# A spectral network's convolutions in quarter tiles of TensorE, with the complex products summed there or from turned matrices

## The chip, the core and the metric

One core of a Trainium2 chip. The metric is the device time of one execution in microseconds. The engines are TensorE (PE, with its weight loads PEld), VectorE (DVE), ScalarE (ACT), GpSimd (POOL) and SyncE (SP), whose queue issues most of the DMAs. "Partition" is the row of on-chip memory (SBUF, and PSUM for TensorE's results, in banks of 128 partitions by 512 float32).

## What is computed

```python
x = A_x                                    # 1 x 2048 x 512, float32
x = x + A(layernorm(x), w_r, w_i)          # A: irfft2(rfft2(x) * (w_r + i w_i))
x = x + B(layernorm(x), ...)               # B: along the 2048 rows, channel by channel:
x = x + A(layernorm(x), w_r, w_i)          #   y = irfft(rfft(u, 4096) * rfft(K, 4096))[:2048] + u * D_skip
x = x + B(layernorm(x), ...)               #   K = 2 Re sum_n C[d, n] exp(dt A[d, n])^position
```

The B layer is a long convolution. Its kernel K (512 channels, 2048 positions, 128 terms each) depends on the parameters alone and is the same in both B layers.

## The kernel before

**The stages**, by the times of the profiled execution: to 76 us the input is normalized and K's parameters are made; to 250 the first A layer runs beside the first half of K; to 456 the second half of K runs beside blocks 0 and 1 of the first B layer; to 546 the rest of that layer; to 663 the second A layer; to 785 the second B layer.

**K in time** (`kernel_time`) goes by 64 half-units in eight groups. `grow` makes powers (`mag`), `bend` multiplies phases on TensorE and rounds them on VectorE (L840, into `kw`), `sine` and `cosine` are ScalarE's (L805), `terms` multiplies on VectorE (L859, L861, into `qp`), `total` sums on TensorE (L872, into `pv`). ScalarE copies the sums to `stage` (L879), and after the last half of a group four DMAs write `stage` to `kt` in DRAM (L883, 128 KB each, SP's queue).

**A convolution** (`forward_b`, `layer_b`) goes by four blocks of 128 channels. Steps of a block:
- `rows`, four times: the first stage of the Fourier transform, small matmuls of 64 x 64 tiles (in the trace `p<-t,w` and `p<-t,x`), copied by ScalarE to `z` (L651).
- `turn`, eight times: VectorE transposes `z` in 32 x 32 pieces (L657).
- `pair` and `weigh`, four times: for each of two planes (real and imaginary part) two or three matmuls of 64 columns with a constant matrix from `mb` (`p<-z,mb`, one PSUM bank a plane) give 16 frequencies of a channel on each half of the partitions; VectorE multiplies each plane by both planes of the kernel's spectrum `kk` (L963, four products into `wb`), and two sums of 64 partitions each make the complex product in `u` (L975, on GpSimd or VectorE as the tables YB and YC say: "v" is VectorE). Frequency 0 and the one at half the rate, both real, are packed in one element that is multiplied apart (L965, with `kf0`).
- `units`, eight times: 16 matmuls (`p<-mb,u`, 64 columns, 64 elements moved) go back through the inner stage; ScalarE copies to the second `u` (L984 to L988). A small one (L983, matrix MIX) sets right the packed element.
- `rows` back, four times: eight matmuls (`p<-u,t`, 64 columns, 128 elements moved) and VectorE's sum with the residual (L1002, into `za` or `xw`); in the first B layer it also takes the statistics of the next layer norm (L1007).

`kernel_freq` (F) takes K through the same forward steps, block by block. ScalarE copies its planes to `kk` (L926), VectorE sets the packed element apart (L934 to L936), and `kk` goes to DRAM as `kf` (L938, SP's queue). In the first B layer the product reads the tiles `kk` where F left them; in the second they are loaded from `kf`, two DMAs of 256 KB a step.

**What sets the order.** `interleave` merges lists of steps by their place in each list; `layer_b` writes the order of a block's steps out by hand, with K's steps between them (`fill`). A scheduler then sets each engine's order of instructions from the program order and its own estimates. Tiles rotate through pools (`w`, `wb`, `kk`, `u`, `qp`, PSUM's `p1`, `p2`, `p3`): a tile's next use waits until the last reader of the earlier one is done. `p2`, which holds the pair's results, has three banks in most of the first B layer and in the second.

Of the kernel before, what the change touches and what calls it, by code (L numbers as in the profile page):

```python
# [12 lines left out]
ALU = mybir.AluOpType  # L13
# [8 lines left out]
WW = 8  # L22
DQ = ''
# [5 lines left out]
LAGV = 4  # L29
# [21 lines left out]
MAG = 4  # L51
TH = 2
QP = 5
KF = 1
PM = '2,3,0'
WB = 7
YB = 'vgggvggg'
YC = 'vgggvgggvgvgvgvv'
# [27 lines left out]
def constants():  # L86
# [18 lines left out]
    out["tbt"] = (T * (2 / 4096)).transpose(4, 3, 0, 2, 1).reshape(128, 32 * 64)  # L105
# [71 lines left out]
    MB = np.zeros((2, 2, 32, 2, 2, 2, 32))  # L177
    MBT = np.zeros((2, 2, 32, 2, 2, 32))
    MIX = np.zeros((2, 2, 32, 2, 2, 32))
    for dq in range(2):  # L180
        for sp, m in enumerate((M0, M)):
            MB[:, dq, :, sp, :, dq, :] = m.reshape(2, 32, 2, 8, 2, 2).transpose(4, 2, 3, 5, 0, 1).reshape(2, 32, 2, 32)
        MBT[:, dq, :, :, dq, :] = M.transpose(0, 1, 3, 2)
        MIX[:, dq, :, :, dq, :] = mix.transpose(2, 3, 0, 1)
    out["mb"] = np.concatenate([MB.reshape(128, 256), MBT.reshape(128, 128), MIX.reshape(128, 128)], 1)

    k0 = (np.arange(128) % 32 == 0).astype(float)[:, None]
    out["kc"] = np.concatenate([k0, 1 - k0], 1)
# [61 lines left out]
class Net:  # L250
# [22 lines left out]
    @contextmanager  # L273
    def phase(self, name, space=bass.MemoryType.SB, side="left", **tags):

        with self.tc.tile_pool(name=name, bufs=1, space=space, side=side, reuse_waits="tile") as pool:
            for tag, v in tags.items():
                self.tags[tag] = self.tags[v] if isinstance(v, str) else (pool, tag, *v)
            yield
        for tag in tags:  # L280
            del self.tags[tag]

# [103 lines left out]
    def layer_a(self, w, x=None, src=None, dst=None):  # L386
# [76 lines left out]
        def spread_four(n0):  # L463
# [5 lines left out]
            g = [self.even[:, i, n0:n0 + 4] for i in range(2)]  # L469
# [13 lines left out]
            for i in range(4):  # L483
                t = self.sb("kk", [128])
# [143 lines left out]
    def forward_b(self, src, T, tag="z", extra=None):  # L628
# [5 lines left out]
        def rows(n0):  # L634


            if n0 == 0:
# [3 lines left out]
            products = [(ps[b][64 * c:64 * c + 64, :, j, m], xs[2 * m + c][64 * b:64 * b + 64, 64 * j:64 * j + 64],  # L641
                         T[64 * b:64 * b + 64, n0 + 2 * m + c].rearrange("p (u r) -> p u r", r=2))
                        for m in range(2) for j in range(2) for c in range(2) for b in range(2)]
            if extra and n0 == 0:
                e = extra()
                for j in (1, 0):
                    products.insert(4 * j + 1, (ps[0][0:64, :, j, 0], e[:, 64 * j:64 * j + 64], products[0][2], True))
# [11 lines left out]

        MB = split(self.small[:, 0:256], "slm", [2, 2, 64])  # L660

        def pair(i, use):
            last = None
            for pl in range(2):
                p = self.ps("p2", [512])
                products = []
                for h in (1, 0):
                    o = p[64 * h:64 * h + 64].rearrange("p (u d) -> p u d", d=32)
                    u = 32 * (i % 2) + 16 * h
                    c = 1 if u == 0 else 0  # L670
                    z = tiles["zt"][:, :, i // 2]
                    products += [(o[:, 0], MB[:, 0, pl], z[:, 0])] * c + [(o[:, c:], MB[:, 1, pl], z[:, u + c:u + 16])]
# [227 lines left out]
    def kernel_freq(self, blk, kt, d_skip, kf, kept, T):  # L900

        nc = self.nc
        m0, m1 = self.kc[0:64, 0:1], self.kc[0:64, 1:2]
# [16 lines left out]
        rows, turns, pairs = self.forward_b(src, T, extra=skip)  # L920

        def keep(i):
            k = kept[blk, i] = [self.sb("kk", [512]) for pl in range(2)]

            def use(pl, p):
# [302 lines left out]
```

## Time and profile before

| | |
|---|---|
| median of the runs | 787.68 us (786.29 to 788.17) |
| the profiled execution | 786.58 us, of which its span 784.8 |
| mean granted TensorE clock | 0.899 |
| largest busy times | PE 612.4, DVE 646.6, ACT 420.4, POOL 415.4 us |
| DMA | 80.26 MB, mean 102 GB/s |

A profile's times are in microseconds from the start of the span, a single instruction's in ns. Its rows name line, engine, operation, output and inputs, and the shapes as partitions x elements. A granted clock of 0.9 means that the throttle let TensorE run at 0.9 of its full rate. Float32 matmuls leave two records each in the trace; 128*64 in front of a shape is the tile of TensorE (rows * columns).

### The profile page before, as it was taken

To read this page: it belongs to the slowest core of one execution; us is meant where nothing else is said; L and a number is where in the kernel's file an instruction comes from. 1 tells how busy PE (TensorE), PEld (TensorE's weight loads), DVE (VectorE), ACT (ScalarE), POOL (GpSimd) and SP (SyncE) were. 2 spreads that over 40 slices of the span, in tenths; PEclk is the share of its full clock that TensorE was granted. 3 is DMA by queue.
4 is the path that set the end of the run, shared out by engine and by line. 5 is a ranking of instruction groups with operands and counts; after the bars stand their busy time and mean duration, and the time that the engine had idled before them with its cause. 6 is when DMAs were issued, how large, how long until landed. Compare 5 with 4: busy or idle time off the path is not lost. (4 is left out here: it accounts for less than half of the span.)

```text
span 784.8 us, 20886 instructions
## 1 busy us (share of the span) xinstructions
PE 612.4 (78%) x8208; PEld 417.6 (53%) x8208; DVE 646.6 (82%) x1301; ACT 420.4 (54%) x919; POOL 415.4 (53%) x596
## 2 busy tenths in 40 slices
PE   3337788698758687897867977865899897889986
PEld 2336566464424342654343645644877664466666
DVE  7999749889997769968996977878587598789993
ACT  3434788755556676787477833323766335243322
POOL 3675886766625226732675166281055473375850
PEclk9656999998975999899989999997999898799998
DMA  8300651343547232452326359422122004134403
GB/s 320 117 0 1 147 124 49 102 101 129 125 161 148 72 105 49 129 139 79 43 67 146 113 120 252 133 82 81 54 82 83 28 14 147 56 91 128 145 24 105
DMA packets 144257, 80.26 MB, mean 102 GB/s; under 512 B 78656, under 2 KB 123840, under 8 KB 143264
## 3 DMA queue, kind: packets, MB, share of 16 engines
q1 hardware_dynamic: 143904, 78.51, 36.0%
q8 instruction: 65, 1.06, 0.5%
q0 software_dynamic: 256, 0.43, 0.3%
q14 instruction: 32, 0.26, 0.1%
HBM read 54.30 MB, written 25.03 MB: 101 GB/s over the span
## 5 line engine op out<-in xcount | busy, mean ns | idle before, releaser
L975 POOL TENSOR_TENSOR u<-wb,wb 64x512 f32<-64x512 f32 x90 | 137.0, 1523 | 81.2 <-DVE wb L963 74.5
L319 PE MATMUL p<-z,mb 128*64 128x512 f32 (+1 forms) x480 | 104.0, 543 | 13.2 <-DVE wb L963 5.8
L651 ACT COPY z<-p 128x512 f32<-128x512 f32 x96 | 51.5, 595 | 70.5 <-PE p L319 47.0
L861 DVE TENSOR_TENSOR qp<-qp,mag 128x1024 f32<-128x1024 f32 x64 | 83.3, 1305 | 1.2
L963 DVE TENSOR_TENSOR wb<-p,kk 128x512 f32<-128x512 f32 x128 | 80.6, 674 | 4.0 <-PE p L319 4.0
L859 DVE SCALAR_TENSOR_TENSOR qp<-qp,mag 128x256 f32<-128x256 f32 x128 | 63.6, 512 | 18.7 <-ACT qp L805 18.4
L319 PEld LDWEIGHTS p<-mb,u 128*64 128x64 f32 x2048 | 67.6, 146 | 17.9 <-issue 9.6
L319 PE MATMUL p<-mb,u 128*64 128x64 f32 x2048 | 69.9, 231 | 8.6 <-DVE u L975 4.2
L657 DVE STREAM_TRANSPOSE z<-z 128x512 f32<-128x512 f32 x96 | 58.5, 673 | 21.1 <-ACT z L651 21.1
L1087 POOL TENSOR_SCALAR w<-w,norms 128x128 f32<-128x128 f32 x64 | 37.8, 604 | 62.7 <-DMA w<-h 59.7
L530 DVE TENSOR_TENSOR w<-wt,p 128x514 f32<-128x514 f32 x64 | 42.5, 687 | 32.4 <-PE p L319 24.2
L535 POOL TENSOR_TENSOR w<-w,w 64x257 f32<-64x257 f32 x48 | 40.0, 834 | 53.7 <-DVE w L530 45.8
L872 PEld LDWEIGHTS pv<-qp 128*32 128x32 f32 x2048 | 38.0, 120 | 53.8 <-issue 20.2
L805 ACT ACTIVATE kf<-pk 128x512 f32<-128x512 f32 x64 | 38.8, 606 | 48.7 <-PE pk L841 48.4
L459 PE MATMUL p<-w,w 128*128 128x128 f32 x128 | 32.1, 429 | 40.6 <-DVE w L452 30.9
L319 PEld LDWEIGHTS p<-z,mb 128*64 128x64 f32 x480 | 34.4, 142 | 50.5 <-issue 30.9
L319 PE MATMUL p<-t,w 64*64 64x128 f32 x1024 | 48.1, 309 | 16.7 <-DMA w<-kt 8.1
L872 PE MATMUL pv<-qp 128*32 128x64 f32 x2048 | 51.6, 240 | 8.2 <-DVE qp L861 5.3
L988 ACT COPY u<-p 128x512 f32<-128x512 f32 x64 | 37.4, 589 | 38.1 <-PE p L319 38.1
L840 DVE TENSOR_SCALAR kw<-pk 128x512 bf16<-128x512 f32 x64 | 43.0, 679 | 13.3 <-PE pk L839 13.3
L319 PEld LDWEIGHTS p<-t,w 64*64 64x64 f32 x1024 | 36.8, 152 | 29.0 <-DMA w<-kt 10.7
L459 PEld LDWEIGHTS p<-w,w 128*128 128x128 f32 x128 | 27.8, 318 | 44.6 <-issue 24.7
(198 smaller groups left out, 1498.1 us busy)
## 6 DMA issues: line engine op xcount, KB each, us to landing
wt<-in_w SPq DMA_DIRECT2D x32, 257.0 KB
kf<-kk SPq DMA_DIRECT2D x32, 256.0 KB
kk<-kf SPq DMA_DIRECT2D x32, 256.0 KB
u<-in_x SPq DMA_DIRECT2D x16, 256.0 KB
hr<-in_x SPq DMA_DIRECT2D x16, 256.0 KB
kt<-stage SPq DMA_DIRECT2D x32, 128.0 KB
h<-hr SPq DMA_DIRECT2D x16, 256.0 KB
w<-kt SPq DMA_DIRECT2D x32, 128.0 KB
```

The costliest lines, as they stand in the source:

```text
L319: last = self.nc.tensor.matmul(out, weights, data, start=not more, stop=True, skip_group_check=True).ins
L459: nc.tensor.matmul(p[:, b], xf[:, b], t, start=True, stop=True)
L530: nc.vector.tensor_mul(m[pl], W, px[:, None, :].to_broadcast([128, 2, 257]))
L535: e[0].tensor_sub(Y[0:64, v], m[0][hs, 0], m[1][hs, 1])
L651: nc.scalar.copy(tiles["z"][:, :, :, b, m:m + 2].rearrange("p u j m r -> p (u j) (m r)"), ps[b].rearrange("p u j m r -> p (u j) (m r)"))
L657: nc.vector.transpose(tiles["zt"][:, u:u + 8].rearrange("p u j d -> p (u j d)"), tiles["z"][:, u:u + 8].rearrange("p u j b m r -> p (u j b ...
L840: nc.vector.tensor_scalar(whole, p, MAGIC, -MAGIC, op0=ALU.add, op1=ALU.add)
L859: nc.vector.scalar_tensor_tensor(QP[:, c, 0], QP[:, c, 1, :, ::-1], -1.0 if c else 1.0, m[:, 0], op0=ALU.mult, op1=ALU.mult)
L861: nc.vector.tensor_mul(t, t, mag[:, None, 1:3, 256 * j:256 * j + 256].to_broadcast([128, 2, 2, 256]))
L872: nc.tensor.matmul(p[32 * t:32 * t + 32, g], QP[:, c, 2, d], QP[:, c, 0:2, d], start=c == 0, stop=c == 1, tile_position=(0, 32 * t), skip_ ...
L963: nc.vector.tensor_mul(split(m[c, pl], "du", [32, 16]), by_channel(p), split(k[c], "du", [32, 16]))
L975: self.added = e[0].tensor_sub(y[0:64], v[0, 0], v[1, 1]), e[1].tensor_add(y[64:128], v[0, 1], v[1, 0])
```

## The change

**Layout.** The planes now alternate by row: the real and the imaginary part of a frequency lie on neighbouring partitions, so that one tile of 128 partitions holds two channel halves (`q`) or row halves (`j`) of both planes. Every matmul of a convolution works in a quarter of TensorE, 64 x 64 (the forward rows in 64 x 32), and a step writes two PSUM banks where it wrote one.

**The complex product.** In the first B layer (`ADD` False) each result of a pair is multiplied by two versions of the spectrum, real parts in both rows of a couple and imaginary parts in both, straight into two tiles `M[0]` and `M[1]`, and the sum is left to TensorE: `units` accumulates two matmuls, with the matrices `MT[0]` and `MT[1]`. In the second (`ADD` True) a second set of matmuls with turned matrices (`TWI`, i times the first) is multiplied by the imaginary parts, and GpSimd adds the two products, 128 partitions at once. `kk` is loaded from `kf` with each row twice (a stride of 0), four DMAs a step, in both B layers; only block 3 of the first takes the tiles that F left (there the matrices, `DUP`, double the rows). YB and YC, and VectorE's sums, are gone. The packed element is handled by ScalarE (`first`) and GpSimd.

**Queues and buffers.** `DQ = 'TaUa'` puts the stores of `kt` and `kf` on ScalarE's queue. `kw` has one buffer (two before), `qp` four (five), `total` lags three halves (four), `w` four tiles (seven); rows back take eight rows at a time (four). `layer_b`'s order of steps is written anew.

| instructions in the program | before | after |
|---|---|---|
| matmuls | 4394 | 6590 |
| of these `mb,u` | 1024 | 1536 |
| back, `u,t` | 256 (of 64 x 128) | 1024 (of 64 x 64) |
| forward, `t,w` and `t,x` | 768 | 1536 |
| VectorE | 1303 | 1225 |
| sums of the complex product, GpSimd | 90 (64 x 512) | 32 (128 x 512) |
| loads of `kk` from `kf`, 256 KB | 32 | 112 |

The diff, without the constants' construction:

```diff
-DQ = ''
+DQ = 'TaUa'
-LAGV = 4
+LAGV = 3
-QP = 5
+QP = 4
-WB = 7
-YB = 'vgggvggg'
-YC = 'vgggvgggvgvgvgvv'
+WB = 4
+ADD = False, True
...
-        def pair(i, use):
+        def pair(i, use, kinds):
+            z = tiles["zt"]
             last = None
-            for pl in range(2):
-                p = self.ps("p2", [512])
+            for x, K in enumerate(kinds):
+                ps = [self.ps("p2", [512]) for q in range(2)]
                 products = []
...
+                for first in (1, 0) if i == 0 else (0,):
+                    us = slice(16 * i, 16 * i + 1) if first else slice(16 * i + (i == 0), 16 * i + 16)
+                    for j in range(2):
+                        for q in range(2):
+                            o = ps[q][64 * j:64 * j + 64].rearrange("p (u d) -> p u d", d=32)[:, us.start - 16 * i:us.stop - 16 * i]
+                            products.append((o, K[64 * q:64 * q + 64, 1 - first], z[64 * q:64 * q + 64, us, j]))
                 last = self.side_by_side(products, last)
-                use(pl, p)
-            self.paired = last
+                for q in range(2):
+                    use(x, q, ps[q])
...
-            for pl in range(2):
-                self.dma("U")(kf[blk, i, pl], k[pl])
+                self.dma("U")(kf[blk, i, q], k[q])
...
+                        part = kf[blk, i, q].rearrange("(r c) f -> r c f", c=2)[:, x]
+                        part = bass.AP(tensor=part.tensor, offset=part.offset, ap=[part.ap[0], [0, 2], part.ap[1]])
+                        self.dma("W")(k[x][q], part)
+                        if i == 0:
+                            nc.gpsimd.tensor_copy(split(k[x][q], "du", [32, 16])[:, :, 0], self.kf0[:, blk, q, x])
             m = {}
...
+            def use(x, q, p):
+                p = by_channel(p)
+                for o in (x,) if own or add else range(2):
+                    y = M[o][:, q, :, 16 * i:16 * i + 16] if not add else split(self.sb("wb", [512]), "du", [32, 16])
+                    f = k[q] if own else k[o][q]
+                    nc.vector.tensor_mul(y, p, split(f, "du", [32, 16]))
+                    m[o, q] = y
+                if add and x == 1:
+                    eng.tensor_add(M[0][:, q, :, 16 * i:16 * i + 16], m[0, q], m[1, q])
...
+            def units(d):
+                ps = [self.ps("p3", [64, 8]) for j in range(2)]
+                self.side_by_side([(ps[j][64 * q:64 * q + 64, :, i], m[64 * j:64 * j + 64, q, d + i],
+                                    self.MT[64 * j:64 * j + 64, x], *[True] * x)
+                                   for i in range(8) for x, m in enumerate(M) for j in range(2) for q in range(2)])
+                for j in range(2):
+                    nc.scalar.copy(V[:, :, j, d:d + 8], ps[j])
...
-            steps = [[now[0], *turns, *last[:2]], [now[1], *last[2:4], *then[1][:1], *last[4:6]],
-                     [now[2], *last[6:], *then[1][1:2], *units[:2]], [now[3], *units[2:4], *then[1][2:], *then[2][:4]]]
+            steps = [now[0], *last[:1], *special, now[1], *last[1:], now[2], *then[1][:2], now[3], *then[1][2:]]
+            turns = then[2]
+            for n in range(4):
+                steps += [*units[n:n + 1], *turns[2 * n:2 * n + 2]]
...
-                early.enter_context(net.phase("k", side="right", kb=(4096, 1), ni=(256, 1), kw=(1024, 2), th=(1536, TH), mag=(6144, MAG),
+                early.enter_context(net.phase("k", side="right", kb=(4096, 1), ni=(256, 1), kw=(1024, 1), th=(1536, TH), mag=(6144, MAG),
```

Where instructions stand, at three places. Names end in the program's running numbers; `order` rows give output, inputs and shape, or for DMAs the pieces.

VectorE in block 0 of the first B layer, amid K's steps (`qp`, `kw`). Before:

```order
L963 TENSOR_TENSOR wb_3299<-p_722_3295,kk_2956 128x512
L963 TENSOR_TENSOR wb_3301<-p_722_3295,kk_2957 128x512
L963 TENSOR_TENSOR wb_3307<-p_725_3303,kk_2956 128x512
L840 TENSOR_SCALAR kw_3316<-pk_3317 128x512
L840 TENSOR_SCALAR kw_3326<-pk_3327 128x512
L965 TENSOR_TENSOR wb_3307<-p_725_3303,kf_1_65 64x32
L963 TENSOR_TENSOR wb_3310<-p_725_3303,kk_2957 128x512
L963 TENSOR_TENSOR wb_3334<-p_734_3331,kk_2977 128x512
L963 TENSOR_TENSOR wb_3336<-p_734_3331,kk_2978 128x512
L963 TENSOR_TENSOR wb_3341<-p_737_3338,kk_2977 128x512
L975 TENSOR_TENSOR u_3264<-wb_3299,wb_3310 64x32x16
L859 SCALAR_TENSOR_TENSOR qp_3321<-qp_3321,mag_3197 128x256
```

After (L1003 is the product, L893 and L891 are L861 and L859, L872 is L840):

```order
L1003 TENSOR_TENSOR u_3391<-p_724_3435,kk_3423 128x32x16
L893 TENSOR_TENSOR qp_2507<-qp_2507,mag_2331 128x2x512
L1003 TENSOR_TENSOR u_3392<-p_724_3435,kk_3425 128x32x16
L1003 TENSOR_TENSOR u_3391<-p_725_3436,kk_3424 128x32x16
L1003 TENSOR_TENSOR u_3392<-p_725_3436,kk_3426 128x32x16
L893 TENSOR_TENSOR qp_2560<-qp_2560,mag_2363 128x2x512
L872 TENSOR_SCALAR kw_2699<-pk_2700 128x512
L891 SCALAR_TENSOR_TENSOR qp_2622<-qp_2622,mag_2363 128x256 x2
L1003 TENSOR_TENSOR u_3391<-p_743_3493,kk_3485 128x32x16
L1003 TENSOR_TENSOR u_3392<-p_743_3493,kk_3487 128x32x16
```

A sum of 64 partitions (L975) and a small product (L965) stood among the products; now they are gone, the products write `u` themselves, and one rounding into `kw` stands where two followed each other.

TensorE in the second B layer, where units of one block meet pairs of the next. Before:

```order
L319 MATMUL p_1660_8206<-mb_2788,u_7827 64x64 x16
L319 MATMUL p_1661_8224<-mb_2788,u_7827 64x64 x16
L319 MATMUL p_1670_8264<-mb_2788,u_7827 64x64 x16
L319 MATMUL p_1671_8282<-mb_2788,u_7827 64x64 x16
L319 MATMUL p_1679_8347<-z_8169,mb_2788 64x512
L319 MATMUL p_1679_8347<-z_8169,mb_2788 64x32
L319 MATMUL p_1679_8347<-z_8169,mb_2788 64x480
L319 MATMUL p_1682_8355<-z_8169,mb_2788 64x512
```

After:

```order
L335 MATMUL p_1732_10311<-mb_2805,u_9262 64x64 x2
L335 MATMUL p_1733_10348<-mb_2805,u_9262 64x64 x2
L335 MATMUL p_1756_10547<-z_10307,mb_2805 64x512
L335 MATMUL p_1757_10548<-z_10307,mb_2805 64x512
L335 MATMUL p_1756_10547<-z_10307,mb_2805 64x512
L335 MATMUL p_1757_10548<-z_10307,mb_2805 64x512
L335 MATMUL p_1760_10557<-z_10307,mb_2805 64x512
L335 MATMUL p_1781_10705<-t_8841,x_8845 32x64x2
```

Before, a plane's matmuls filled one bank `p`; now the four of a step go to two banks in turn, and units and forward rows alternate between two banks as well.

ScalarE at the end of a K group (L805 and L837 are sines, cosines and powers; L879 and L911 the copies to `stage`). Before:

```order
L879 COPY stage_3485<-pv_3694 128x64x2
L805 ACTIVATE mag_3772<-pk_3773 128x512
L805 ACTIVATE mag_3772<-pk_3779 128x512
L879 COPY stage_3485<-pv_3731 128x64x2
L805 ACTIVATE mag_3813<-pk_3814 128x512
L805 ACTIVATE mag_3813<-pk_3820 128x512
L879 COPY stage_3485<-pv_3782 128x64x2
L805 ACTIVATE mag_3823<-pk_3824 128x512
L926 COPY kk_3942<-p_849_3944 128x512
```

After:

```order
L837 ACTIVATE mag_3394<-pk_3401 128x512
L837 ACTIVATE mag_3413<-pk_3414 128x512
L911 COPY stage_2668<-pv_3366 128x64x2
L915 DMA kt<-stage_2668 2048x1x16 x4
L837 ACTIVATE mag_3413<-pk_3420 128x512
L837 ACTIVATE mag_3449<-pk_3450 128x512
L837 ACTIVATE mag_3449<-pk_3456 128x512
L837 ACTIVATE kf_3465<-pk_3460 128x512
```

After the last copy to `stage` the four stores of `kt` now stand on this queue, ahead of the next group's activations.

More of the change, by code (lines that the diff above doesn't have):

```diff
@@ L920, in kernel_freq @@
         rows, turns, pairs = self.forward_b(src, T, extra=skip)
+        first = self.first
         def keep(i):
[L923 to L936 removed]
```

240 lines of the change are left out of this document (128 added, 112 removed).

## The prediction

> **What bounds the kernel now.** I read the page's busy times first, then the busy time by stage, then VectorE's groups by shape in the three stages that hold the convolutions, then TensorE's timeline for what one matmul costs. The first fence holds the page's VectorE line and the table by stage; behind the stage and its length stand busy microseconds and instructions of PE, PEld, DVE, ACT and POOL, the granted clock, the DMA share and GB/s.
>
> ```profile
> PE 612.4 (78%) x8208; PEld 417.6 (53%) x8208; DVE 646.6 (82%) x1301; ACT 420.4 (54%) x919; POOL 415.4 (53%) x596
> 0.00:250.00 250.00, 171.84 (x1593) 119.60 (x1594) 215.68 (x475) 146.34 (x322) 156.08 (x278) 0.84 0.41 115
> 250.00:456.00 206.00, 167.13 (x2903) 94.12 (x2906) 176.10 (x299) 143.59 (x283) 97.65 (x104) 0.91 0.38 99
> 456.00:546.00 90.00, 61.83 (x1086) 46.12 (x1078) 69.61 (x150) 28.89 (x60) 46.16 (x47) 0.93 0.50 138
> 546.00:663.00 117.00, 108.30 (x751) 82.19 (x750) 89.31 (x223) 62.78 (x180) 53.12 (x122) 0.95 0.21 63
> 663.00:785.00 122.00, 103.27 (x1888) 75.57 (x1888) 95.89 (x156) 38.83 (x76) 62.35 (x45) 0.92 0.32 94
> ```
>
> The fourth stage is the second A layer, which the change leaves alone. In the second (K's last groups beside blocks 0 and 1) VectorE is busy 176 of 206 us: it leads, and what it does is worth its time. In the third (block 2, F of block 3, block 3) and the last (the second B layer) VectorE has 70 of 90 and 96 of 122 us, TensorE 62 and 103: neither is full, and they wait for each other in turn. So a microsecond taken from VectorE there is worth less than one. The groups that the change touches, by stage (busy, mean of one, idle ahead):
>
> ```profile
> L861 DVE TENSOR_TENSOR qp<-qp,mag 128x1024 f32<-128x1024 f32 x40 | 51.5, 1292 | 1.1
> L859 DVE SCALAR_TENSOR_TENSOR qp<-qp,mag 128x256 f32<-128x256 f32 x79 | 40.1, 523 | 12.2 <-ACT qp L805 11.9
> L975 DVE TENSOR_TENSOR u<-wb,wb 64x512 f32<-64x512 f32 x8 | 7.0, 880 | 0.0
> L936 DVE TENSOR_SCALAR kk<-kk,kc 64x32 f32<-64x32 f32 x6 | 2.3, 385 | 0.0
> L934 DVE TENSOR_SCALAR kf<-kk,kc 64x32 f32<-64x32 f32 x6 | 2.1, 354 | 1.1 <-ACT kk L926 1.1
> L935 DVE SCALAR_TENSOR_TENSOR kf<-kk,kc,kf 64x32 f32<-64x32 f32 x6 | 1.5, 254 | 0.1
> L965 DVE TENSOR_TENSOR wb<-p,kf 64x32 f32<-64x32 f32 x4 | 0.8, 193 | 0.0
> ...
> L657 DVE STREAM_TRANSPOSE z<-z 128x512 f32<-128x512 f32 x24 | 14.6, 676 | 11.2 <-ACT z L651 11.2
> L975 DVE TENSOR_TENSOR u<-wb,wb 64x512 f32<-64x512 f32 x11 | 14.5, 1321 | 0.2
> L935 DVE SCALAR_TENSOR_TENSOR kf<-kk,kc,kf 64x32 f32<-64x32 f32 x2 | 1.5, 758 | 0.0
> L934 DVE TENSOR_SCALAR kf<-kk,kc 64x32 f32<-64x32 f32 x2 | 1.1, 528 | 1.7 <-ACT kk L926 1.7
> L965 DVE TENSOR_TENSOR wb<-p,kf 64x32 f32<-64x32 f32 x4 | 0.8, 200 | 0.1
> L936 DVE TENSOR_SCALAR kk<-kk,kc 64x32 f32<-64x32 f32 x2 | 0.5, 241 | 0.0
> ...
> L963 DVE TENSOR_TENSOR wb<-p,kk 128x512 f32<-128x512 f32 x64 | 40.2, 675 | 3.7 <-PE p L319 3.7
> L975 DVE TENSOR_TENSOR u<-wb,wb 64x512 f32<-64x512 f32 x19 | 24.8, 1307 | 0.3
> L1002 DVE TENSOR_TENSOR za<-za,p 128x512 f32<-128x512 f32 x16 | 10.4, 674 | 9.4 <-PE p L319 9.3
> L965 DVE TENSOR_TENSOR wb<-p,kf 64x32 f32<-64x32 f32 x8 | 1.6, 204 | 0.3
> ```
>
> The reader is to see that L975, a sum of half the partitions, costs 1.3 us where it reads SBUF beside GpSimd and 0.88 us elsewhere, twice a product that reads PSUM (0.675), and that these sums go.
>
> **TensorE: smaller matmuls.** What one record costs is the difference of two bursts of the same form, so that the latency drops out (an f32 matmul leaves two records).
>
> ```profile
> 689.79 2.10 PE L319 MATMUL p<-mb,u 128*64 128x64 f32 x66
> 405.06 1.15 PE L319 MATMUL p<-mb,u 128*64 128x64 f32 x32
> 691.81 1.10 PE L319 MATMUL p<-t,x 64*64 64x128 f32 x32
> 646.34 0.67 PE L319 MATMUL p<-t,x 64*64 64x128 f32 x16
> 711.18 2.84 PE L319 MATMUL p<-u,t 128*64 128x128 f32 x48
> 716.55 1.09 PE L319 MATMUL p<-u,t 128*64 128x128 f32 x16 [1.49 <-DVE za L1002]
> 433.78 0.39 PE L872 MATMUL pv<-qp 128*32 128x64 f32 x12
> 437.47 0.65 PE L872 MATMUL pv<-qp 128*32 128x64 f32 x32
> 698.99 1.08 PE L319 MATMUL p<-z,mb 128*64 128x512 f32 x4
> 691.81 0.20 PEld L319 LDWEIGHTS p<-t,x 64*64 64x64 f32 x7
> ```
>
> Units: (2.10 - 1.15)/34 = 27.9 ns. Forward rows: 0.43/16 = 26.9. Rows back: 1.75/32 = 54.7. K's summing matmuls (32 columns of the array, 64 moved): 0.26/20 = 13.0. One plane of a pair: 1.08 us. A block of the second B layer has 8 planes (8.6 us), 256 records of units (7.1), 64 of rows back (3.5) and 128 forward (3.4): 22.7 us. After it has 8.6 for the pairs (twice the matmuls, on a quarter each) and three times 256 records. No row shows a 64x64 quarter with 64 moved, or a 64x32 one with 128. The nearest rows bound them: 13.0 ns (pv, which also moves 64) and 27 ns (t,x, whose tiles are quarters too). I take 13, since pv is nearest in size and seven weight loads on quarter tiles begin within 0.20 us, 29 ns or less each, while several tiles work: 3.3 us for each 256, so 18.6 us a block against 22.7. At 27 it is 29.5 us.
>
> The Trainium skill has a rule against this, in "TensorE: Matmul & The Clock Gate", section "Back-to-back issue gap": 1 to 64 moved columns cost an issue floor of about 25 ns. "TensorEngine Tiling (Array Packing)", section "Instruction Overhead", says the same as some 60 cycles each, and warns against taking the tiling factor from a dimension that is already small. By it the small matmuls would come out at the 27 ns end. The pv row, at 13.0 ns start to start, disagrees for 32-column tiles; no run here yet shows it for quarters.
>
> **The second B layer (663 to 785).** Gone from VectorE: L975 x19, 24.8 us, and L965 x8, 1.6 us; products, transposes and residual adds keep their count and size. The sums go to GpSimd, 32 of 128x512:
>
> ```profile
> L975 POOL TENSOR_TENSOR u<-wb,wb 64x512 f32<-64x512 f32 x90 | 137.0, 1523 | 81.2 <-DVE wb L963 74.5 <-DVE wb L965 1.4
> L1063 POOL TENSOR_TENSOR t<-za 128x512 f32<-128x512 f32 x8 | 11.1, 1420 | 0.1
> ```
>
> 32 x 1.42 = 45 us, within a stage of 122, and less than it had (62 us). What is late next: a product step now fills two banks of three where it filled one. Its successor starts when VectorE has freed the first, needs up to 1.08 us, and VectorE has one product of 0.675 left: 0.4 us of stall, at some 20 of 32 steps (the others have a transpose or residual add between): +8. Between two halves TensorE's in-order queue holds a unit or a rows step (0.8 us at 13 ns, 1.8 at 27); where one stands ahead of a half, half a microsecond at 16 of 32 places: +8. The last sum before the units is one of 1.42 on GpSimd: +1. Together -26.4 + 17 = -9. Ends: -20 (stalls a third of that) and +8 (stalls twice).
>
> **456 to 546.** L975 x11 goes, 14.5 us, and L934, L935, L936 and L965, 3.9 us; ScalarE and GpSimd copy element 0 instead, with 54% and 53% busy. VectorE already waited 11.2 us here for z, which a faster VectorE makes longer; two banks a step and, without adders, twice the unit matmuls (512 records a block: 6.7 us at 13 ns, against 7.1) come on top: +8. So -10, ends -16 and 0.
>
> **250 to 456.** L975 x8 goes (7.0), L934 to L936 and L965 (6.7), and L861 and L859 lose some GpSimd beside them: 91.6 us, of which I take 4. So -18. Against it, the stores of `kt` and `kf` move from SP's queue to ScalarE's:
>
> ```profile
> 289.86 4.95 SPq L883 DMA_DIRECT2D kt<-stage  x4
> 280.31 0.35 SPq L938 DMA_DIRECT2D kf<-kk  x1
> ACT kf L805 <- PE pk L841: 23.9, 15, 4.3
> ```
>
> Four issues at a K group's end hold the queue 4.95 us, and the next group's sines (L805, on which VectorE's L859 already waited 11.9 us) stand behind them. ScalarE's waiting for TensorE (23.9 us) is slack that can take some. By the order of the changed kernel, at two of the four boundaries VectorE has nothing of the convolution to do: 2 x 5 = 10; at the others 1.5 each; of 24 `kf` issues at 0.35 (8.4 us) I charge a half. +17, so -1. Ends -12 (slack takes nearly all) and +15 (all reach the path: 4 x 4.95 + 8.4 = 28, and smaller buffers 5). The single `kw`, the smaller `qp` and the shorter lag cost nothing as long as VectorE has convolution work between two of L840, which the order shows.
>
> **0 to 250.** Three or four such bursts beside a layer that reads the same input: +2, ends 0 and +10.
>
> **The loads of the spectrum.** 32 become 112 of 256 KB, all on SP's queue, which lost the stores. Second B layer:
>
> ```profile
> kk<-kf SPq DMA_DIRECT2D x32, 256.0 KB
> GB/s 215 5 0 0 0 121 76 158 172 109 68 0 66 123 163 130 75 188 289 23 9 171 177 1 171 177 207 142 0 5 0 0 0 170 175 10 5 0 228 116
> ```
>
> 64 of the loads are 16.8 MB, the result 4.2, the table 2: 23 MB, 80 us at the 289 GB/s of the best slice (estimate: if all slices could reach it), 153 at 150 GB/s, near the mean of its busier slices. They are asked for two pairs ahead, so I take them as hidden: 0, ends 0 and +25 (153 less the stage's 122, some of it fetched before).
>
> **Sum.** -9 - 10 - 1 + 2 = -18 against the profiled execution's 786.58 us (span 784.8 and 1.8 around it), so 768.6. The median of the runs is 787.68, 1.1 higher, and the profiled execution lies within their 786.29 to 788.17; I say 769.
>
> **Rivals.**
> 1. *All of VectorE's freed time comes out*: 24.8 + 1.6 + 14.5 + 3.9 + 7.0 + 6.7 = 58.5 us, so 729, and half way 757. For it: VectorE has the most busy time in every stage but one, and the stalls above are worked out, not seen. Against: its waits for z and p (11.2, 9.3 us) show that TensorE and ScalarE are close behind. Chance 0.16.
> 2. *Slower by ScalarE's queue*: 8 x 4.95 + 32 x 0.35 = 51 us of issuing stand on ScalarE; I have charged 19. From 37 us on the path the kernel is slower than before; all of it gives 801. For it: VectorE already waits 11.9 us for L805, so a late sine is seen. Against: ScalarE is busy 144 of 206 us in that stage, and 23.9 us of the rest is waiting for TensorE that an issue can fill. Chance 0.12.
> 3. *Slower by the issue of small matmuls*: at 27 ns a block of the last layer takes TensorE 29.5 us, four 118 of the stage's 122, and with its waits for z and p some 10 more than now; units of the first B layer grow from 7.1 to 14 us in four blocks, half of it seen. About +14 to +25 instead of -18: 800 to 812. Between 13 ns and 27 the sum changes its sign at about 20. The skill's floor of the same section is this rival. Chance 0.05, as the pv row speaks against it.
> 4. *Slower by the loads*: at 150 GB/s VectorE waits 25 us in the last stage: 794 to 815. Chance 0.04.
> 5. *Little remains*: stalls at their upper ends, 781 to 785.3: 0.07; no difference, 785.3 to 790: 0.06.
>
> **How the numbers follow.** The forecast, 757 to 781, has 0.50. Faster by over 0.3%, about what a measurement of this kernel can tell from no change, is 0.50 + 0.16 + 0.07 = 0.73; within it 0.06; slower 0.12 + 0.05 + 0.04 = 0.21. The range goes from 748, which leaves out the better half of rival 1, to 796, which leaves out rival 3, most of 4 and the worst of 2: some 0.2 in all.
>
> **What would show it.** In the last stage VectorE busy about 70 us, no sum on it, waits of its products for p grown from 3.7 to 15 us or more, and units of 64 records in under 1.1 us (right) or 1.7 (rival 3). At a K group's end four stores on ScalarE's queue and behind them L859's successor waiting for the sine 3 us and more (right at two places, rival 2 at all). VectorE's products waiting for kk by DMA would be rival 4. I would be wrong if TensorE's time by record does not fall, or if a stage that gains passes its gain on as a longer wait for z.

## The result, and the profile after

The changed kernel takes 904.31 us (median of 4 runs, 902.01 to 908.96) against 786.98 for the kernel before: ratio 1.1504, 95% interval 1.1443 to 1.1564. It is 117 us slower where 18 less were forecast, and lies far outside the range. Times here and below are medians of all executions; the ratios leave out executions in a slower state that a few fall into.

The page's busy times, and the table by stage of the changed kernel (columns as in the prediction; the stages are cut at the same events: first half of K and first A layer, K's second half, rest of the first B layer, second A layer, second B layer, give or take the last rows of block 3):

```profile
PE 665.2 (74%) x12600; PEld 422.5 (47%) x12600; DVE 584.9 (65%) x1223; ACT 419.7 (47%) x919; POOL 313.2 (35%) x570
0.00:266.00 266.00, 181.50 (x1865) 126.66 (x1865) 215.19 (x479) 145.12 (x321) 153.87 (x287) 0.81 0.42 120
266.00:520.00 254.00, 181.99 (x4407) 96.98 (x4407) 158.39 (x272) 146.89 (x291) 50.79 (x98) 0.78 0.44 120
520.00:632.00 112.00, 79.28 (x2255) 49.01 (x2247) 39.18 (x81) 22.65 (x46) 10.32 (x10) 0.79 0.37 102
632.00:755.00 123.00, 107.25 (x881) 81.90 (x873) 99.56 (x261) 69.62 (x193) 56.15 (x132) 0.96 0.24 74
755.00:901.00 146.00, 115.18 (x3216) 68.00 (x3216) 72.58 (x133) 35.45 (x69) 42.05 (x44) 0.85 0.46 144
```

VectorE's work fell as planned (585 us for 647, 72.6 for 95.9 in the last stage), yet every stage became longer: by 16, 48, 22, 6 and 24 us against the table of the prediction, which forecast +2, -1, -10, 0 and -9. No engine is full in any of them. The waits say where. VectorE and ScalarE between 266 and 520 us, then VectorE in the last stage (us in total, times, longest):

```profile
DVE kw L872 <- PE pk L871: 38.1, 10, 10.6
DVE xw L1046 <- PE p L335: 35.1, 4, 10.7
DVE qp L891 <- ACT qp L837: 17.5, 26, 3.0
ACT mag L837 <- DMA kt<-stage: 21.7, 4, 7.0
DVE wb L1003 <- PE p L335: 30.8, 23, 4.3
DVE za L1046 <- PE p L335: 20.6, 5, 13.5
```

Three things stand behind these rows. First, the end of a K group. Timelines of ScalarE's queue, ScalarE and VectorE:

```profile
323.50 4.79 ACTq L915 DMA_DIRECT2D kt<-stage  x4
328.34 1.09 ACT L837 ACTIVATE mag<-pk 128x512 f32<-128x512 f32 x2 [4.87 <-DMA kt<-stage]
318.74 1.22 DVE L893 TENSOR_TENSOR qp<-qp,mag 128x1024 f32<-128x1024 f32 x1
330.10 0.69 DVE L872 TENSOR_SCALAR kw<-pk 128x512 bf16<-128x512 f32 x1 [10.13 <-PE pk L871]
```

The four stores hold ScalarE for 4.8 us; the powers `mag` of the next group, TensorE's L862 and L871 and VectorE's rounding stand behind them, and VectorE is idle for 10.1 us. Second, TensorE, whose matmuls come in batches:

```profile
549.16 2.97 PE L335 MATMUL p<-mb,u 64*64 64x64 f32 x128 [2.19 <-issue]
555.63 3.69 PE L335 MATMUL p<-mb,u 64*64 64x64 f32 x128 [3.50 <-issue]
...
616.71 2.13 PE L335 MATMUL p<-mb,u 64*64 64x64 f32 x128 [0.80 <-issue]
620.19 2.09 PE L335 MATMUL p<-mb,u 64*64 64x64 f32 x128 [1.35 <-issue]
623.68 1.39 PE L335 MATMUL p<-mb,u 64*64 64x64 f32 x77 [1.39 <-issue]
```

The table by stage for these stretches (the last columns are the granted clock, the share of the DMA engines and GB/s):

```profile
545.00:549.00 4.00, 1.97 (x128) 1.84 (x128) 4.00 (x8) 1.07 (x2) 0.00 (x0) 1.00 0.87 239
549.00:555.00 6.00, 2.97 (x128) 2.79 (x128) 0.49 (x1) 1.07 (x2) 0.00 (x0) 0.59 1.02 244
614.00:624.00 10.00, 6.45 (x403) 6.04 (x399) 0.00 (x0) 3.22 (x6) 1.34 (x2) 1.00 0.02 5
```

A batch of 128 records runs in 2.1 us at full clock, 16 ns a record, near the 13 that I took (in 2.97 and 3.69 us where the granted clock was 0.59 and 0.50). Then TensorE stands still, waiting for nothing that the profile shows ("issue"). From batch to batch it is 3.5 us in the quiet stretch at 614 us, and 4.28 us from 544.88 to 549.16, at full clock, where other transfers fill the DMA engines; the 6.47 us that follow have both the transfers and the lower clock, so what they owe to which is open. Third, steps that fill both banks of `p1`, so that TensorE and the engines that read it take turns; L1046's waits are read so here, and run 5 tests it.

### The profile page after: what moved, and what is told of

Its sections match the earlier page's. It is cut to its first block, busy times and chain, and to the rows that moved or that the text cites. A ratio compares the mean times of both kernels' runs of the same rounds, so it can differ in the third digit from the quotient of the medians.

```text
span 900.5 us, 29679 instructions
## 1 busy us (share of the span) xinstructions
PE 665.2 (74%) x12600; PEld 422.5 (47%) x12600; DVE 584.9 (65%) x1223; ACT 419.7 (47%) x919; POOL 313.2 (35%) x570
## 3 DMA queue, kind: packets, MB, share of 16 engines
q8 instruction: 99, 1.62, 0.7%
## 5 line engine op out<-in xcount | busy, mean ns | idle before, releaser
L335 PE MATMUL p<-z,mb 64*64 64x512 f32 (+2 forms) x744 | 139.1, 635 | 24.1 <-DVE u L1003 11.8
L335 PE MATMUL p<-mb,u 64*64 64x64 f32 x3072 | 65.9, 236 | 22.3 <-issue 13.8
L893 DVE TENSOR_TENSOR qp<-qp,mag 128x1024 f32<-128x1024 f32 x64 | 80.2, 1254 | 2.0
L335 PEld LDWEIGHTS p<-mb,u 64*64 64x64 f32 x3072 | 59.9, 148 | 32.7 <-issue 19.6
L872 DVE TENSOR_SCALAR kw<-pk 128x512 bf16<-128x512 f32 x64 | 43.7, 683 | 44.8 <-PE pk L871 42.9
L891 DVE SCALAR_TENSOR_TENSOR qp<-qp,mag 128x256 f32<-128x256 f32 x128 | 54.0, 440 | 22.5 <-ACT qp L837 21.5
L1003 DVE TENSOR_TENSOR wb<-p,kk 128x512 f32<-128x512 f32 x64 | 41.3, 685 | 41.1 <-PE p L335 30.8
L335 PEld LDWEIGHTS p<-z,mb 64*64 64x64 f32 x744 | 34.8, 161 | 68.3 <-issue 27.9
L335 PE MATMUL p<-t,w 64*32 64x128 f32 x2048 | 53.9, 315 | 13.7 <-issue 6.3
L837 ACT ACTIVATE kf<-pk 128x512 f32<-128x512 f32 x64 | 39.1, 610 | 49.4 <-PE pk L873 42.6
L1006 POOL TENSOR_TENSOR u<-wb,wb 128x512 f32<-128x512 f32 x32 | 39.9, 1274 | 62.6 <-DVE wb L1003 33.4
L1003 DVE TENSOR_TENSOR u<-p,kk 128x512 f32<-128x512 f32 x64 | 40.3, 683 | 32.9 <-PE p L335 24.6
L335 PEld LDWEIGHTS p<-t,w 64*32 64x32 f32 x2048 | 38.7, 118 | 34.3 <-issue 16.3
```

Of the source, the lines that this page charges most:

```text
L335: last = self.nc.tensor.matmul(out, weights, data, start=not more, stop=True, skip_group_check=True).ins
L837: last["x"] = nc.scalar.activation(*a, **k).ins
L872: nc.vector.tensor_scalar(whole, p, MAGIC, -MAGIC, op0=ALU.add, op1=ALU.add)
L891: nc.vector.scalar_tensor_tensor(QP[:, c, 0], QP[:, c, 1, :, ::-1], -1.0 if c else 1.0, m[:, 0], op0=ALU.mult, op1=ALU.mult)
L893: nc.vector.tensor_mul(t, t, mag[:, None, 1:3, 256 * j:256 * j + 256].to_broadcast([128, 2, 2, 256]))
L1003: nc.vector.tensor_mul(y, p, split(f, "du", [32, 16]))
```

## The experiments

Each time stands beside runs of the kernel before on the same chip (786 to 792 us).

**1. The stores back on SP's queue** (changed kernel, `DQ = ''` for `'TaUa'`).

> The changed kernel with DQ = '', so that the stores of kt and kf are issued by SP's queue again; nothing else differs. Theory Q (ScalarE's queue): in the changed kernel's trace each of the K groups from 160 us on ends with four stores on ScalarE's queue, 4.8 to 6.9 us, and the next group's powers, the matmuls L862 and VectorE's rounding L872 wait behind them (10.1 us of VectorE at 320). Seven such ends at 5 to 6 us each: 35 to 42 us less, so 860 to 870. Theory M (number of matmuls, and the instructions that TensorE must be sent): no more than 10 us less, 893 to 903, since the waits only change their name.

897.88 us, ratio 1.1389 (1.1312 to 1.1466): 9 us less by the ratios, with intervals that overlap, which is theory M's number. The queue alone does not carry the loss. In its trace (an execution of 909 us) VectorE's waits between 257 and 522 us are now these:

```profile
DVE xw L1046 <- PE p L335: 33.7, 2, 17.1
DVE xw L1046 <- DMA xw<-h: 20.1, 2, 10.2
```

The time of the queue went over to the residual sums: the load of `xw` waits on the same queue behind the store of the eight rows before, and the stores of `kt` and `kf` now stand there too.

**2. Two buffers of xw** (changed kernel).

```diff
-XW = 1
-ST = 2
+XW = 2
+ST = 1
-folds: fa=(4096, 2)
+folds: fa=(4096, 1)
```

> The changed kernel with two buffers of xw where it has one; the memory comes from stage (one buffer for two) and fa (one for two). Theory X (the single xw): VectorE's residual sum of a block's second eight rows waits 7.5 us in blocks 0 and 1 and 3.5 in block 2, because the load of xw waits for the store of the eight rows before. With two buffers these go: 15 to 18 us less, 885 to 890. Rival: the sum then waits for TensorE's rows instead (L1046's waits are put down to PE by the profile), and less than 5 us come out.

902.10 us, ratio 1.1494 (1.1404 to 1.1584): nothing, as the rival had it. The sum of the second eight rows still waits for TensorE (6.1 and 6.3 us where it waited 7.5).

**3. The matmuls cut, in the kernel before.**

```diff
-  (p[64 * r:64 * r + 64, :, i], Y[:, j, d + i], MBT[:, 64 * r:64 * r + 64]) ... for r in range(2)
+  (p[64 * r + h:64 * r + h + 32, :, i], Y[:, j, d + i, h:h + 32], MBT[:, 64 * r:64 * r + 64]) ... for r in range(2) for h in (0, 32)
```

and in the same way the forward rows and the rows back.

> The kernel before with its small matmuls cut in two by columns of TensorE: units and rows back in 32 columns instead of 64, forward rows in 32 instead of 64; 6256 matmuls in TensorE's list for 4200 (the changed kernel has 6396), and the same work, buffers, queues and order of steps. Theory M: TensorE cannot be sent that many instructions at the rate that the array could take (in the changed kernel's trace TensorE stands still for 1.4 to 3.5 us, put down to issue, after nearly every 128 records of a long row of small matmuls): slower by 20 to 50 us, 807 to 837. Theory Q and X: less than 8 us, 780 to 795, since a record costs 13 to 16 ns after the cut and 27 before it.

834.28 us, ratio 1.0614 (1.0553 to 1.0676): 48 us slower with the same work, at the upper end of theory M. TensorE's waits for issue in the kernel before, then in this one; then the transfers of instructions on queue 8 (packets, MB, share) of the kernel before, the changed one, and this one:

```profile
PE p L319 <- issue: 8.6, 9, 3.7
...
PE p L319 <- issue: 32.7, 30, 3.7
```

```profile
q8 instruction: 65, 1.06, 0.5%
...
q8 instruction: 99, 1.62, 0.7%
...
q8 instruction: 97, 1.59, 0.8%
```

The changed kernel's 12600 matmul records and as many weight loads are 25200 instructions; 1.62 MB over them is 64 bytes each, and a packet of 16.4 KB holds 256, which is 128 matmuls with their weight loads: the length of a batch. The kernel before fits as well (16416 instructions, 1.06 MB, 65 packets). So queue 8 brings TensorE its program. The packets' own times, which the trace has one by one, agree: in the changed kernel 26 of TensorE's 27 waits for issue (32.3 of 32.9 us) end 1.2 to 1.6 us after such a packet has ended; in the kernel before it is 2 of 9 (4.7 of 8.6 us), in this one 24 of 30 (29.8 of 32.7 us). These standstills grew by 25 us, of the 48 that the edit costs. TensorE's busy time grew as well, from 612.4 to 633.7 us, though each matmul is half as large: 118 records of cut units take 1.88 us, 15.9 ns each, where half of 27.9 would be 14.0. How the two add up to 48 was not tried.

**4. The stores on ScalarE's queue, in the kernel before** (`DQ = 'TaUa'`).

> The kernel before with DQ = 'TaUa', so that the stores of kt and kf are issued by ScalarE's queue; nothing else differs. Theory Q: 30 to 45 us slower, 817 to 832, as each K group's end stops ScalarE for 5 us and more. Rival (the stores hurt only together with the smaller buffers and the lost cover by the convolution's work): 0 to 15 us slower, 787 to 802.

820.97 us, ratio 1.0445 (1.0385 to 1.0505): 35 us slower, theory Q. ScalarE's wait and VectorE's between 250 and 500 us, and VectorE's in the kernel before (250 to 456):

```profile
ACT mag L805 <- DMA kt<-stage: 25.5, 4, 11.2
DVE kw L840 <- PE pk L839: 17.3, 6, 6.9
...
DVE kw L840 <- PE pk L839: 9.4, 3, 4.7
```

**5. Two banks a step, in the kernel before.** Both planes of a pair, two units steps and two rows steps are taken together, their matmuls alternating between two banks:

```diff
-                p = self.ps("p3", [64, 8])
-                self.side_by_side([(p[64 * r:64 * r + 64, :, i], Y[:, j, d + i], MBT[:, 64 * r:64 * r + 64])
-                                   for i in range(8) for r in range(2)])
+                ps = [self.ps("p3", [64, 8]) for k in range(2)]
+                self.side_by_side([(ps[k][64 * r:64 * r + 64, :, i], Y[:, j, d + 8 * k + i], MBT[:, 64 * r:64 * r + 64])
+                                   for i in range(8) for r in range(2) for k in range(2)])
```

> The kernel before, with each step of pairs, units and rows back on two PSUM banks whose matmuls alternate, as the changed kernel has them: both planes of a pair together, two units steps as one, two rows steps as one. Same matmuls (64 columns), same work, queues and buffers. Theory B (lost double buffering): between 250 and 456 us p1 has two banks, which a step now fills alone, and p2 has three; ScalarE's and VectorE's reading no longer runs beside the next step's matmuls: 20 to 40 us slower, 807 to 827. Rival: other work fills the gaps, and less than 8 us come out of it.

815.62 us, ratio 1.0308 (1.0239 to 1.0377): 24 us slower, theory B. (The edit also makes a step twice as large, so that other work finds fewer places between steps; the run does not separate the two.) ScalarE's wait for the forward rows between 250 and 470 us, in the kernel before between 250 and 456, and VectorE's wait for rows back in this one's last stage:

```profile
ACT z L651 <- PE p L319: 20.5, 10, 5.5
...
ACT z L651 <- PE p L319: 6.5, 8, 2.4
...
DVE za L1008 <- PE p L319: 18.2, 3, 14.2
```

**6. Cut, queue and banks together, in the kernel before.**

> The kernel before with three edits at once: the cut of the matmuls by columns (alone 48 us slower), the stores on ScalarE's queue (alone 35 us slower) and the two banks a step. If these three carry the changed kernel's loss and add up, with 20 to 40 us for the banks: 890 to 905, the changed kernel's 904 with none of its new arithmetic. If they share the same waits: 845 to 870, and the rest is for the changed kernel's own order of steps, its single buffers and its loads.

894.46 us, ratio 1.1311 (1.1252 to 1.1371): 103 us, where the three alone add up to 107. They hardly share waits.

**7. The stores on SP's queue and two buffers of xw** (changed kernel; edits 1 and 2).

> The changed kernel with both edits of the first two runs on it: the stores on SP's queue and two buffers of xw. With the queue alone VectorE waits 20 us for the load of xw by DMA between 257 and 522 us and 34 for TensorE at the same instructions, and the forward rows wait behind it for their PSUM banks. Theory X (each hides the other): 25 to 45 us less than the changed kernel, 860 to 880. Rival (TensorE's instructions bound this stage whatever waits): as with the queue alone, 890 to 900.

882.69 us, ratio 1.1072 (1.0988 to 1.1157): 34 us less by the ratios (0.0432 of 787), 28 by the medians, where the two alone gave 9 and 1. Its executions spread from 873 to 889 us, so the size is rough; that it is more than 10 is clear. Theory X: each hid the other. VectorE no longer waits for `xw` by DMA; TensorE's row stays as it was:

```profile
DVE xw L1046 <- PE p L335: 33.7, 4, 17.0
```

**8. A row of small matmuls by itself.** Behind the last sum of the kernel before:

```diff
+        ps = [net.ps("p3", [8, 64]) for q in range(2)]
+        net.side_by_side([(ps[q][64 * j:64 * j + 64, i % 8], h[64 * q:64 * q + 64, 15, 384 + 64 * j:448 + 64 * j], T[64 * q:64 * q + 64, i % 16, 0:64])
+                          for i in range(128) for j in range(2) for q in range(2)])
```

> The kernel before with 512 more matmuls behind its last sum (1024 records), in 64 x 64 quarters with 64 elements moved, in a row with nothing to wait for and no transfers but the last stores; what they give is used nowhere. Theory M (TensorE's instructions come in blocks of 128 records, 256 instructions, and a block takes about 3.5 us to come): the row takes 1024 x 27 ns = 28 us or more with a standstill after each 128, although single records start 16 ns apart, and the time is 814 or more. Rival (the array sets the rate): 16 us without standstills, 802 to 805.

814.04 us, ratio 1.0288 (1.018 to 1.0396). TensorE's timeline, and the table by stage for its end:

```profile
793.38 2.10 PE L319 MATMUL p<-t,za 64*64 64x64 f32 x128 [1.82 <-issue]
796.85 2.10 PE L319 MATMUL p<-t,za 64*64 64x64 f32 x128 [1.38 <-issue]
800.32 2.10 PE L319 MATMUL p<-t,za 64*64 64x64 f32 x128 [1.38 <-issue]
804.07 2.10 PE L319 MATMUL p<-t,za 64*64 64x64 f32 x128 [1.65 <-issue]
...
800.00:817.90 17.90, 9.76 (x586) 9.07 (x586) 0.00 (x0) 0.00 (x0) 0.00 (x0) 1.00 0.02 5
```

A batch of 128 starts every 3.47 to 4.0 us and runs for 2.1, at full clock, with the other engines idle: 28.3 us for the 1024 records (788.65 to 816.95), 27.6 ns each over the row and 15 inside a batch. From 796 to 817 us the only transfers are six packets of queue 8; here are the rates in slices of 0.525 us, and the queue:

```profile
GB/s 0 0 0 31 0 0 0 0 0 0 31 0 0 0 0 0 0 31 0 0 0 0 0 0 0 31 0 0 0 0 0 0 31 0 0 0 0 0 0 31
q8 instruction: 6, 0.10, 2.2%
```

One packet comes for each batch, and the whole program has eight packets more than the kernel before (73 for 65), as 2048 more instructions should. A packet starts 1.07 to 1.16 us after a batch of 128 has begun and takes 0.95 to 1.40 us, and the next batch begins 1.27 to 1.50 us after its end. This is theory M without any kernel around it, in the profiled execution (819.73 us). The other execution took 808.34 us, about what the rival gives on this chip (15 to 18 us over the 791.5 of the kernel before): a row of 28.3 us fits into it only if all that stands before the row ended some 5 us earlier than in the fastest of the seven runs of the kernel before. So the mechanism is seen in the trace, and the two times alone decide nothing.

**9. No reload in the first B layer** (changed kernel).

```diff
-            own = kept is not None and blk == 3
+            own = kept is not None
```

> The changed kernel with every block of the first B layer taking the tiles kk where F left them, as block 3 does: the 48 loads of kk from kf in that layer (12.6 MB) go, and the matrices double the rows. As many matmuls but for element 0. Theory H (the loads were hidden, as predicted): 0 to 10 us less, 894 to 904; 8 us is what VectorE waited for them by DMA at 528 to 537. Rival (the loads slow the blocks of TensorE's instructions too: 4.0 to 6.5 us a block at 545 to 576, where transfers run, for 3.5 without): 15 to 30 us less, 874 to 889.

923.52 us, ratio 1.1711 (1.1645 to 1.1777): 19 us slower than the changed kernel, which neither theory had. Leaving the loads out brings no time back. Perhaps F's tiles, held until the products, delay what follows; this is not shown, and which wait carries it was not tried.

**10. Edits 1, 2 and 9 together** (changed kernel).

> The changed kernel with three edits: the stores on SP's queue, two buffers of xw, no reload in the first B layer. Theory M: what is left of the loss is the cut of the matmuls (48 us) and the two banks (24), less what VectorE's sums gave: 850 to 870, still 7 to 10% slower than before. Rival: without these waits the saved work of VectorE comes out, and the time falls below 830.

880.32 us, ratio 1.1137 (1.1056 to 1.1219): as run 7, which has the same edits and the 48 loads. What is left is not in the queue or `xw`, and leaving those loads out does not take it away; whether they cost some time that holding F's tiles takes back is not separated.

**11. VectorE's sums left out, in the kernel before** (the 38 of L975 that YB and YC put on VectorE).

> The kernel before without the 38 sums of 64 partitions that VectorE makes (L975); those of GpSimd stay, and u is filled with zeros once in each B layer. It leaves out part of the complex product, to see what the freed time of VectorE (7.0 + 14.5 + 24.8 = 46 us) is worth by itself. By my prediction's steps, with stalls counted apart: nearly all, 740 to 750. Rival (VectorE shares the lead with TensorE, ScalarE and GpSimd, and its wait for them grows instead): 10 to 25 us less, 762 to 777.

777.29 us, ratio 0.9862 (0.9806 to 0.9917): 11 of 46 us, the rival. VectorE's waits over the whole span, here and in the kernel before:

```profile
DVE z L657 <- ACT z L651: 33.4, 11, 5.9
DVE za L1004 <- PE p L319: 22.6, 7, 11.2
DVE wb L964 <- PE p L319: 12.4, 9, 4.1
...
DVE z L657 <- ACT z L651: 21.1, 8, 4.5
DVE za L1002 <- PE p L319: 16.8, 5, 8.8
DVE wb L963 <- PE p L319: 4.0, 5, 1.5
```

Much of the freed time turned into waits for z (+12), for rows back (+6) and for the pairs (+8).

**12. Four banks for the pairs of the last layer** (changed kernel; p2 four, p3 two).

> The changed kernel with four PSUM banks for the pairs of the second B layer (p2) where it has three, and two for units and rows back (p3) where it has three. My prediction charged 8 us for products that wait for the second bank. If that is what VectorE's 31 us of waiting for p in that stage are: 8 to 15 us less, 889 to 896. Rival (they are TensorE's instructions that come late): within 5 us of the changed kernel, 899 to 909.

904.70 us, ratio 1.1449 (1.137 to 1.1527): no difference that can be told. Last stage, this kernel and then the changed one:

```profile
DVE wb L1003 <- PE p L335: 10.8, 11, 2.4
DVE wb L1003 <- POOL u L1006: 20.8, 3, 11.3
...
DVE wb L1003 <- POOL u L1006: 3.2, 1, 3.2
```

The products' wait for p fell from 30.8 to 10.8 us, and those for GpSimd's sums rose from 3.2 to 20.8. The edit takes a bank from units and rows back, so it may cost there what it gives to the pairs; what the second bank is worth by itself it does not tell.

**13. K's smaller buffers, in the kernel before.**

```diff
-LAGV = 4
+LAGV = 3
-QP = 5
+QP = 4
-kw=(1024, 2)
+kw=(1024, 1)
```

> The kernel before with K's smaller buffers: qp four for five, kw one for two, total three halves behind for four. My prediction gave them nothing as long as VectorE has convolution work between two roundings. If so: within 5 us of before, 783 to 793. Rival (they lengthen the chain from ScalarE's sine to VectorE's product at each half): 10 to 25 us slower, 798 to 813.

805.71 us, ratio 1.0186 (1.0129 to 1.0243): 15 us, the rival. VectorE's wait between 250 and 478 us, 9.4 in the kernel before:

```profile
DVE kw L840 <- PE pk L839: 19.6, 6, 6.9
```

Its two longest waits (5.48 us to 310.62 and 6.86 us to 438.01) end 1.1 and 4.1 us after the stores of a group have started (309.52 and 433.95): at the ends of two groups. Which of the three buffers carries it was not tried.

**14 and 15. All four edits, and the same without VectorE's sums, in the kernel before** (edits of 6 and 13; then 11).

> The kernel before with the cut matmuls, ScalarE's queue, two banks a step (103 us together) and K's smaller buffers. If the buffers cost nothing beside the other three: 887 to 899. If they add 10 to 25 us as in the rival of the run before: 900 to 920.

> The same four edits, and VectorE's 38 sums left out (part of the complex product is missing, u is filled with zeros once in each B layer). If the freed time of VectorE still comes out as it does alone (11 us): 11 us under the run before. Rival (TensorE's instructions and ScalarE's queue lead by then): within 5 us of it.

903.52 us, ratio 1.1461 (1.1359 to 1.1564), and 895.85, ratio 1.1324 (1.1256 to 1.1393). The buffers add up. The sums' gain is 8 us by the medians and 11 by the ratios, with intervals that overlap: these runs do not tell whether it shrinks.

Where the time lies, from each trace (us; the second column is ScalarE's last copy to `stage`, the third the last sum of the second A layer):

| | K ends | second A ends | end of span |
|---|---|---|---|
| before | 455.6 | 661.3 | 784.8 |
| changed | 520.5 | 753.8 | 900.5 |
| 3: cut | 468.9 | 683.4 | 830.9 |
| 4: ScalarE's queue | 500.5 | 697.5 | 823.6 |
| 5: two banks | 471.1 | 670.7 | 812.9 |
| 13: buffers | 478.2 | 682.7 | 806.0 |
| 14: all four | 527.0 | 744.6 | 898.3 |
| 15: the same without sums | 528.3 | 747.5 | 891.3 |

The queue and the buffers cost in K (45 and 23 us to its end). The cut costs in the last stage above all: 148 us from the second A layer's end to the end of the span for 124 before, as long as the changed kernel's 147. The banks cost in both (16 and 19 more) and gain 6 between. Set against run 15, which lacks VectorE's sums as the changed kernel does, the changed kernel is longer between K's end and the second A layer's (233 us for 219): there, between 520 and 632 us, VectorE waits 8.3 us for `kk` and 3.5 for `xw` by DMA.

## Why the prediction was wrong

- **The small matmuls: the step that failed most.** 13 ns a record came from bursts of 12 and 32 records, all inside one batch. Inside a batch it was a little too low (15 to 16 ns). Over the long row of run 8 it was 27.6 ns, set by the arrival of the program and not by the array, so what counts is the number of instructions: 25200 for 16416, weight loads with them (6396 and 4200 matmuls in the traces; the table ahead of the prediction counts 194 more for both). That the rate came out at rival 3's 27 ns is chance: the rival had a price for each record, and this one is for each packet. Its chance was 0.05, and its price, 14 to 25 us, was too low: 48 for the cut alone. The sign that was to decide between the two, 64 records of units in under 1.1 us or in 1.7, came out on the forecast's side (128 in 2.1 us) and was blind to the standstill behind them. The weight loads of one burst could not show it either; the kernel before has two standstills behind a packet (4.7 us), and the prediction read neither. The floor of about 25 ns that the Trainium skill gives in "TensorE: Matmul & The Clock Gate", section "Back-to-back issue gap", is close to the rate over a row (27.6); inside a batch the traces disagree with it (15). The Trainium skill, in "Runtime: NRT & Kernel Launch", section "Instruction fetch mechanics", has the blocks: programs are fetched 16 KiB, 256 instructions, at a time, which agrees with the packets above. It calls the cost of a crossing mostly hidden; the standstills of 0.8 to 3.5 us disagree.
- **ScalarE's queue: the right mechanism, half the size.** I charged 19 of 51 us; alone it costs 35. The burst of 4.95 us was priced by itself; behind it stands a chain (powers, two matmuls, rounding), so VectorE lost 10.1 us at one end of the changed kernel, and ScalarE waited up to 11.2 us for one burst in run 4. The rival's point of decision, 37 us, was nearly reached by the queue alone.
- **Smaller buffers: charged at nothing, 15 us in the kernel before.** I named as cover the convolution work between two roundings; run 13's longest waits, at the ends of two groups, say that it is missing there.
- **Two banks: the size by luck.** I charged 8 for the second bank, 8 for TensorE's order and 8 for the third stage; alone the banks cost 24. By run 5's trace the last stage has 19 for my 16, but another 16 lie up to K's end, where I had charged none, and the part between is 6 shorter where I had charged 8.
- **VectorE's freed time: the gain was not there.** I counted it nearly whole in three stages, with stalls apart. Alone the sums (46 us) are worth 11: the idle behind z and rows back, quoted in the prediction, was the sign that other engines end just behind VectorE. I had also written that VectorE has the most busy time in every stage but one; by the prediction's own table it is every stage but two, and the last, where most of the work was to go, is one of them (TensorE 103.3 us, VectorE 95.9).
- **The loads: right where I looked.** In the last stage VectorE has no wait for `kk` by DMA. In the third it has 8.3 us of it, rival 4's sign in a stage where no loads were charged; and leaving 48 of them out made nothing faster (runs 9 and 10), as far as an edit that also holds F's tiles can say.

The four edits make 113 us of the kernel before (903.52 less 790.91) and, without the sums, 105; by the ratios 0.146 and 0.132 of the changed kernel's 0.150. The last 0.018, some 14 us, lie in what has no run of its own in the kernel before: its single `xw`, its loads, the order of steps; which of these is open. The granted clock was lower in the changed kernel (0.824 for 0.899), but run 14 is as slow at 0.895, so the bulk of the loss needs no separate cause in the clock; whether the clock has a part in those 14 us was not tried. That the standstills are the fetch of the program rests on the batch's length, the packets' size and number, and their times: nearly every standstill ends just after a packet has come. Why the next packet starts only after a batch has begun is not shown.

## What to carry to other kernels

Count TensorE's instructions, not only its array time: where a stage sends more than about 128 small matmuls in a row, price them at the rate of the fetch (here 3.5 us and more for 128 with their weight loads) and take that rate from a long row, not from a short burst. A DMA's issue on a compute engine's queue costs its own time plus the chain that stands behind it. Before counting an engine's freed time, leave the work out and measure: here a quarter came out.

## What the runs showed of the hardware

- A batch of 128 f32 matmul records with their weight loads is one packet of 16.4 KB on queue 8. In a long row (run 8) a batch began 3.47 to 4.01 us after the one before, at full clock and with nothing else moving: 1.07 to 1.16 us until the packet started, 0.95 to 1.40 for it, 1.27 to 1.50 from its end to the batch. In the third stage of the changed kernel it was 4.28 us at full clock beside transfers.
- Quarter tiles came at 15 ns a record inside a batch (64 x 64, 64 elements moved), where the half tiles of the kernel before took 28.
- Four stores of 128 KB held ScalarE's queue for 4.8 to 6.9 us in the changed kernel, and for up to 11.1 us in run 4; in the kernel before they had held SP's for 4.9 to 6.7.
